# Window attention ahead of two gated MLPs: scores as four 64x64 tiles of TensorE's array, all eight heads of a token tile in one unit

## Chip, core and metric

One core of one Trainium2 chip. The metric is the device time of one execution in microseconds. The kernel before was run three times: 983.77, 983.69 and 981.26, median 983.69.

## What is computed

Attention over a sliding window of 64 tokens (4 batches, 8 heads, 576 tokens, head size 64), then two gated MLPs over the 2304 tokens (model size 512, hidden size 1536), all in float32. The reference, cut:

```python
def _attn_ref(q, k, v):
    scores = scale * np.matmul(q, k.transpose(0, 1, 3, 2))
    rel = pos[:, None] - pos[None, :]
    mask = (rel >= 0) & (rel < window)          # window = 64
    scores = np.where(mask, scores, -1000000000.0)
    ...                                         # softmax over the last axis
    return np.matmul(attn, v)

def _moe_ref(x, w_gate, w_val, w_out):
    gate = 1.0 / (1.0 + np.exp(-(x @ w_gate)))
    return gate * (x @ w_val) @ w_out

def _moe2_ref(x, w_a, w_b, w_out):
    return (x @ w_a) * (x @ w_b) @ w_out
```

## The kernel before

**Work.** The 2304 tokens are 18 token tiles of 128; two tiles make a block of 256 tokens (blocks 0 to 8). Blocks 0 to 4 (FRONT, in the groups 0, 1-2 and 3-4) go through the MLPs as plain products; blocks 5 to 8 (BACK) go through a scheme with seven products for eight in the second half of the program (`quad`, `bank_sum`), which the change does not touch. Each MLP weight is split into a high and a low part, and each product is three matmuls in fp32r. The weights arrive as 64-bit words that `decode` (L277) turns into the two parts: for each of the three pieces a, b, o of a chunk F it needs on ScalarE `low` (L285), `ex` (L288) and the high part (L303), on VectorE `wi`, `ex` and the low part, on GpSimd an addition (L296); the results are also stored to DRAM for the second half (`ka`, `kb`, `ko`, `kf`). There are 24 chunks.

**Attention before.** `attention(t, hq, dst, c0)` (L101) is one unit: token tile t, and half of the heads (hq 0 or 1, four heads), so 36 units. A query block of 64 tokens needs 128 keys: its own 64 and the 64 before, so a token tile of 128 queries has two halves s, and the key tile `kt` holds 64 + 128 columns. The steps of a unit, each ended by a `yield`:

1. load k, q, v of four heads (L110), four transposes on TensorE into one bank `kqps` (L119), which puts two heads on the 128 partitions (head parity e: partitions 0 to 63 and 64 to 127); evict `kt` (L121) and `qt` (L128). `qt` is zero padded: for each half s its 128 columns are 64 queries of the even head with zeros below, and 64 queries of the odd head with zeros above, so ScalarE writes it in two pieces of 64 partitions. Copies of v between partitions go by DMA to `vb` (L135, L139).
2. scores: four full matmuls into one bank, `sps[:, s, j, :] = qt[:, j, s]^T kt` (L146), 128 partitions (parity, query) by 128 keys.
3. and 4. for each s: mask and minimum on VectorE (L155), exp with the row sum on ScalarE (L160).
5. normalise on GpSimd (L169), four transposes `tps` (L172), evict `pt` (L174).
6. for the second half of the heads: attention times v, 16 matmuls of 128 rows by 64 columns with 64 moving columns into `xps` (L187), and the split of the result into `xh` and `xl` (L194, L195), or into `xq` (L198) for BACK blocks.

**Order.** `attention_stream` (L236) advances all live units in turn and starts a new one every `LAG` rounds. `attend(blk)` runs it until a block is done; in the middle of the program `attend(steps=...)` spreads the units of BACK evenly, by `STEPS`. `FIRST` (L442) says what has to be issued before the first products: attention of block 0, weights of chunks 0 and 1, attention of block 1, then products of block 0 with chunks 0 and 1, weights 2, attention 2, products of block 1, and so on. The framework then orders the instructions of each engine by its own timeline, so what is issued early in the program can stand later in an engine's queue. All DMAs are issued from SyncE's queue (SP).

**Memory.** PSUM has eight banks: two in `ps_acc` (tag acc), three in `ps_gv` (gv) and three in `ps_at` (at). `kqps`, `sps`, `tps` and `xps` come from `ps_at`, the first tiles' `kqps` from `ps_acc` and `sps` from `ps_gv`. The loaded words wait in three buffers of `stage`.

Of the kernel before, what the change touches and what calls it, by code (L numbers as in the profile page):

```python
# [9 lines left out]
F32 = mybir.dt.float32  # L10
# [10 lines left out]
def tile_window_attention_gated_mlps(ctx, tc, q, k, v, w1g, w1v, w1o, w2a, w2b, w2o, out):  # L21
# [14 lines left out]
    LAG = 1  # L36
# [18 lines left out]
    kts, vs, work, small = pool("kts", 5), pool("vs", 5), pool("work", 3), pool("small", 5)  # L55
# [10 lines left out]
    mask_0 = qp.tile([P, P], F32, name="mask_0")  # L66
# [12 lines left out]
    nc.vector.tensor_copy(mask_0, mask_n)  # L79
    nc.vector.memset(mask_0[:, 0:WIN], MASKED)  # L80


    lo, hi = slice(0, D), slice(D, P)
    before, own, last = slice(0, WIN), slice(WIN, KW), slice(P, KW)
    prev, held = {}, {}
# [15 lines left out]
    def attention(t, hq, dst, c0):  # L101
# [3 lines left out]
        heads = slice(4 * hq, 4 * hq + 4)  # L105
        raw = {}
        for nm, src in (("k", k), ("q", q), ("v", v)):
            r = (vs if nm == "v" else work).tile([P, 4, D], F32, tag=nm, name=f"{nm}{t}_{hq}")
            for off, n, b, s in runs(t * P, P):
                nc.sync.dma_start(out=r[off:off + n], in_=src[b, heads, s:s + n, :].rearrange("h s d -> s h d"))  # L110
            raw[nm] = r
# [3 lines left out]
        p_kq, p_s = (ps_acc, "acc") if t < 4 else (ps_at, "at"), (ps_gv, "gv") if t < 2 else (ps_at, "at")  # L115
# [4 lines left out]
        kt = kts.tile([P, 2, KW], F32, tag="kt", name=f"kt{t}_{hq}")  # L120
        nc.scalar.activation(out=kt[:, :, own], in_=kqps[:, 0], func=AF.Copy)  # L121
        if starts == [0]:
            nc.vector.memset(kt[:, :, before], 0.0)
        else:
            nc.gpsimd.tensor_copy(kt[:, :, before], prev["k", hq][:, :, last])
        qt = qts[(2 * t + hq) % len(qts)]
# [5 lines left out]
        prev["k", hq] = kt  # L132

        vb = work.tile([P, 4, D], F32, tag="vb", bufs=4, name=f"vb{t}_{hq}")
        nc.sync.dma_start(out=vb[hi], in_=raw["v"][lo])  # L135
        if starts == [0]:
            nc.gpsimd.memset(vb[lo], 0.0)
        else:
            nc.sync.dma_start(out=vb[lo], in_=prev["v", hq][hi])  # L139
        prev["v", hq] = raw["v"]  # L140
# [8 lines left out]
        yield  # L149
        ssum = small.tile([P, 2, 2], F32, tag="ssum", name=f"ssum{t}_{hq}")  # L150
        nmax = small.tile([P, 2, 2], F32, tag="nmax", name=f"nmax{t}_{hq}")
        pr = work.tile([P, 2, 2, P], F32, tag="pr", name=f"pr{t}_{hq}")
        for s in range(2):
            for j in range(2):
# [654 lines left out]
```

## Time and profile before

| | |
|---|---|
| median of 3 runs | 983.69 us (981.26 to 983.77) |
| profiled execution, its own time | 980.67 us |
| its span in the trace | 978.9 us |
| mean granted TensorE clock in the span | 0.997 of 2.4 GHz |

The profile is of a single execution. The span is the time from its first to its last instruction; the 1.8 us between span and time lie around the program. A matmul in float32 shows in the trace as two records on PE and two weight loads on PEld, one in fp32r as one. Starts of records are measured; the ends of matmuls are modelled, so the pace of TensorE is read from starts, or from the chain, in which each piece runs to the end of the last record in it.

### The profile page before, as it was taken

The numbers are of one execution on the slowest core, as the hardware profiler recorded it, in microseconds if no ns is written. First come the engines' busy times: TensorE is split into PE (matmuls) and PEld (weight loads), VectorE is DVE, ScalarE is ACT, GpSimd is POOL, SyncE is SP. The second block draws the span as 40 slices with busy tenths as digits, with TensorE's granted clock in tenths as the row PEclk, the third lists the DMA queues.
The fourth block names the chain that finished last, engine by engine and source line by source line (L and its number), as shares of the span: only waits on it lengthen the run. The fifth ranks groups of instructions, "written<-read, shape, count | busy, mean of one in ns | idle before, by whom it ended". The sixth has DMA issues, their size and how long they took to land.

```text
span 978.9 us, 15471 instructions
## 1 busy us (share of the span) xinstructions
PE 960.2 (98%) x5486; PEld 822.2 (84%) x5486; DVE 594.5 (61%) x1175; ACT 484.7 (50%) x1131; POOL 324.5 (33%) x351
## 2 busy tenths in 40 slices
PE   7799999999999999999999999999999999999998
PEld 6699998888888888888888888888888878888886
DVE  4788569776666794576575374445554674455645
ACT  7998666565454575654443233543332444322221
POOL 3543314332222221222121253543430485434300
PEclk9899999999999999999999999999999999999999
DMA  8999568675465573555462335544344564442312
GB/s 196 267 293 296 166 207 301 199 232 170 150 203 180 186 215 119 162 196 175 129 224 79 120 129 197 179 151 146 112 151 150 174 212 154 150 149 88 108 44 86
DMA packets 126524, 167.47 MB, mean 171 GB/s; under 512 B 63344, under 2 KB 92272, under 8 KB 126448
## 3 DMA queue, kind: packets, MB, share of 16 engines
q1 hardware_dynamic: 126448, 166.49, 53.1%
q8 instruction: 43, 0.70, 0.3%
q14 instruction: 33, 0.27, 0.1%
HBM read 106.95 MB, written 55.05 MB: 165 GB/s over the span
## 4 chain that ended last, share of the span: by engine, by line
PE 89%; ACT 4%; DVE 3%; DMA 1%; issue 1%; POOL 1%; SPq 0%; DVEq 0%; ACTq 0%; POOLq 0%
PE gps L320 16%; PE vps L320 16%; PE qa L609 13%; PE accq L669 13%; PE acc L363 8%; PE accm L408 7%; PE qb L609 6%; PE qc L609 3%; PE sps L146 2%; PE xps L187 2%; ACT pr L160 1%; PE tps L172 1%; PE kqps L119 1%; DMA kf<-ex 1%; ACT qt L128 1%
## 5 line engine op out<-in xcount | busy, mean ns | idle before, releaser
L296 POOL TENSOR_TENSOR wi<-wi,low 128x512 int32<-128x512 int32 x72 | 100.4, 1394 | 316.1 <-DVE wi L293 261.4
L320 PE MATMUL gps<-xh,wa 128*128 128x512 f32 (+1 forms) x624 | 175.6, 350 | 0.3 <-ACT xh L194 0.3
L320 PE MATMUL vps<-xh,wb 128*128 128x512 f32 (+1 forms) x624 | 169.4, 341 | 0.5 <-DVE wb L304 0.5
L594 POOL TENSOR_TENSOR wq<-s,wq 128x256 fp32r<-128x256 f32 x96 | 77.4, 810 | 147.1 <-ACT wq L593 147.0
L320 PEld LDWEIGHTS gps<-xh,wa 128*128 128x128 f32 x624 | 111.4, 191 | 13.9 <-ACT xh L194 0.5
L320 PEld LDWEIGHTS vps<-xh,wb 128*128 128x128 f32 x624 | 110.7, 189 | 14.3 <-DVE wb L304 0.7
L320 PE MATMUL gps<-xl,wa 128*128 128x512 f32 (+1 forms) x312 | 107.3, 344 | 1.1 <-DVE xl L195 1.1
L320 PE MATMUL vps<-xl,wb 128*128 128x512 f32 (+1 forms) x312 | 106.3, 341 | 0.0
L408 PE MATMUL accm<-hh,wo 128*128 128x256 f32 (+1 forms) x336 | 86.4, 332 | 0.0
L673 DVE TENSOR_TENSOR res<-accq,res 128x512 f32<-128x512 f32 x80 | 54.3, 687 | 49.0 <-PE accq L669 48.8
L627 ACT ACTIVATE r<-qa 128x512 f32<-128x512 f32 x72 | 42.6, 594 | 83.6 <-PE qa L609 80.3
L609 PE MATMUL qa<-op,wq 128*128 128x512 f32 x288 | 75.5, 390 | 0.7 <-POOL op L551 0.7
L363 PE MATMUL acc<-wo,hh 128*128 128x512 f32 x240 | 74.6, 392 | 1.4 <-DVE res L673 0.8
L609 PE MATMUL qb<-op,wq 128*128 128x512 f32 x288 | 73.4, 389 | 0.0
L330 DVE SCALAR_TENSOR_TENSOR hl<-hr,hh 128x512 fp32r<-128x512 f32 (+1 forms) x78 | 55.2, 708 | 24.2 <-ACT hh L329 23.9
L298 DVE SCALAR_TENSOR_TENSOR ex<-ex,wi 128x512 f32<-128x512 f32 x72 | 52.9, 735 | 24.6 <-ACT ex L288 13.1
L320 PEld LDWEIGHTS gps<-xl,wa 128*128 128x128 f32 x312 | 59.7, 191 | 7.4 <-DVE xl L195 1.3
L329 ACT ACTIVATE hh<-hr 128x512 fp32r<-128x512 f32 (+1 forms) x78 | 41.3, 529 | 48.8 <-DVE hr L347 30.9
L591 POOL TENSOR_TENSOR s<-wf 128x256 f32<-128x256 f32 x48 | 39.5, 822 | 76.7 <-DMA wf<-kf 75.0
L320 PEld LDWEIGHTS vps<-xl,wb 128*128 128x128 f32 x312 | 59.1, 189 | 6.9
L609 PEld LDWEIGHTS qa<-op,wq 128*128 128x128 f32 x288 | 53.9, 188 | 12.2 <-POOL op L551 1.1
L609 PEld LDWEIGHTS qb<-op,wq 128*128 128x128 f32 x288 | 54.1, 188 | 11.2
(125 smaller groups left out, 2031.8 us busy)
## 6 DMA issues: line engine op xcount, KB each, us to landing
wa<-ka SPq DMA_DIRECT2D x27, 512.0 KB, 3.2
wb<-kb SPq DMA_DIRECT2D x27, 512.0 KB, 3.8
wo<-ko SPq DMA_DIRECT2D x27, 512.0 KB, 4.4
st_o<-in_moe_w_out_dram SPq DMA_DIRECT2D x24, 512.0 KB, 4.2
kf<-ex SPq DMA_DIRECT2D x48, 256.0 KB, 4.0
ka<-wa SPq DMA_DIRECT2D x24, 512.0 KB, 3.0
kb<-wb SPq DMA_DIRECT2D x24, 512.0 KB, 3.5
ko<-wo SPq DMA_DIRECT2D x24, 512.0 KB, 3.2
```

The costliest lines, as they stand in the source:

```text
L296: nc.gpsimd.tensor_tensor(out=wi, in0=wi, in1=low, op=ALU.add)
L298: nc.vector.scalar_tensor_tensor(out=wf, in0=ex, scalar=SMALLEST, in1=wi.bitcast(F32), op0=ALU.is_ge, op1=ALU.mult)
L320: nc.tensor.matmul(ps, lhsT=a[:, c * P:(c + 1) * P], rhs=b[:, c, :], start=(n == 0), stop=(n == 3 * NP - 1))
L329: nc.scalar.activation(out=hh, in_=hr, func=AF.Copy, scale=factor)
L330: nc.vector.scalar_tensor_tensor(out=hl, in0=hr, scalar=factor, in1=hh.bitcast(F32), op0=ALU.mult, op1=ALU.subtract)
L363: nc.tensor.matmul(ps, lhsT=a[:, m * P:(m + 1) * P], rhs=b, start=begin and n == 0 and (phase == 1 or m % 2 == 0), stop=end and n == 2 and ...
L408: nc.tensor.matmul(ps[:, m], lhsT=a[:, sl], rhs=b, start=k == 0, stop=k == total - 1)
L594: nc.gpsimd.tensor_tensor(out=t[:, 1], in0=s, in1=t[:, 0].bitcast(F32), op=ALU.subtract)
L609: nc.tensor.matmul(ps, lhsT=a[:, c * P:(c + 1) * P], rhs=b[:, c, :], start=first and n == 0, stop=n == 5, skip_group_check=True,)
L627: nc.scalar.activation(out=r, in_=ps, func=AF.Copy)
L669: nc.tensor.matmul(ps, lhsT=a, rhs=b, start=n == 0, stop=n == len(pairs) - 1)
L673: nc.vector.tensor_tensor(out=dst, in0=ps, in1=dst, op=ALU.add)
```

## The change

The unit becomes a token tile with all eight heads (18 units, `LAG` 3, eleven steps). A load brings all eight heads (twice the bytes, half as many loads). The keys' transposes go to one bank, the queries' to another, and each is evicted in one ScalarE instruction of 128x512; the queries are no longer padded with zeros. The scores are 16 matmuls of 64 rows (one head's dimensions) by 64 columns (64 queries) with 128 moving columns (keys): the row half is the head's parity e, the column half is s, and the parities write to two banks, `sps[0]` and `sps[1]`. The partitions of the scores, the exps and `tps` are now (s, query) instead of (parity, query). The number and size of the instructions for mask, exp, normalising, transposes, `pt` and `xps` stay; the `xps` matmuls alternate between the two column halves one by one, instead of two by two. The mask for the first tile of a batch is made when it is needed (4 times), not once. Pools get new buffer counts. `STEPS` follows the new number of steps.

```diff
-    LAG = 1
+    LAG = 3
...
-    kts, vs, work, small = pool("kts", 5), pool("vs", 5), pool("work", 3), pool("small", 5)
+    kts, vs, work, small = pool("kts", 2), pool("vs", 3), pool("work", 2), pool("small", 2)
...
-    qts = [qp.tile([P, 2, 2, 2, WIN], F32, name=f"qt{i}") for i in range(2)]
-    for qt in qts:
-        nc.vector.memset(qt[hi, :, :, 0], 0.0)
-        nc.vector.memset(qt[lo, :, :, 1], 0.0)
+    def load_tile(nm, src, t, pool_of, tag, bufs):
+        r = pool_of.tile([P, H, D], F32, tag=tag, bufs=bufs, name=f"{nm}{t}")
+        for off, n, b, s in runs(t * P, P):
+            nc.sync.dma_start(out=r[off:off + n], in_=src[b, :, s:s + n, :].rearrange("h s d -> s h d"))
+        return r
...
-    def attention(t, hq, dst, c0):
+    def attention(t, dst, c0):
+        raw = [load_tile(nm, src, t, work, "kq", 3) for nm, src in (("k", k), ("q", q))]
+        v_own = load_tile("v", v, t, vs, "v", 3)
+        yield
-        kqps = p_kq[0].tile([P, 2, 2, P], F32, tag=p_kq[1], name=f"kqps{t}_{hq}")
-        for i, nm in enumerate("kq"):
-            for j in range(2):
-                nc.tensor.transpose(kqps[:, i, j, :], raw[nm][:, 2 * j:2 * j + 2, :], ident)
+        kqps = [kp.tile([P, NP, P], F32, tag=kq_tag, name=f"{nm}ps{t}") for nm in "kq"]
+        for ps, r in zip(kqps, raw):
+            for j in range(NP):
+                nc.tensor.transpose(ps[:, j, :], r[:, 2 * j:2 * j + 2, :], ident)
...
-        for e, rows in enumerate((lo, hi)):
-            nc.scalar.activation(
-                out=qt[rows, :, :, e], in_=kqps[rows, 1].rearrange("p j (s t) -> p j s t", s=2),
-                func=AF.Copy, scale=QSCALE,
-            )
+        qt = qp.tile([P, NP, P], F32, tag="qt", bufs=2, name=f"qt{t}")
+        nc.scalar.activation(out=kt[:, :, own], in_=kqps[0], func=AF.Copy)
+        nc.scalar.activation(out=qt, in_=kqps[1], func=AF.Copy, scale=QSCALE)
...
-        sps = p_s[0].tile([P, 2, 2, P], F32, tag=p_s[1], name=f"sps{t}_{hq}")
-        for s in range(2):
-            for j in range(2):
-                nc.tensor.matmul(
-                    sps[:, s, j, :], lhsT=qt[:, j, s], rhs=kt[:, j, s * WIN:s * WIN + P], start=True, stop=True
-                )
+        sps = [sp.tile([P, NP, P], F32, tag=s_tag, name=f"sps{t}_{e}") for e in range(2)]
+        for j in range(NP):
+            for turn in range(2):
+                for e, dims in enumerate((lo, hi)):
+                    s = (e + turn) % 2
+                    rows = slice(s * WIN, (s + 1) * WIN)
+                    nc.tensor.matmul(
+                        sps[e][rows, j, :], lhsT=qt[dims, j, rows], rhs=kt[dims, j, s * WIN:s * WIN + P],
+                        start=True, stop=True,
+                    )
...
-    STEPS = 4 * TB * 2 * 7 + 8
+    STEPS = len(BACK) * TB * 11 + 8
```

How the engines' queues change is shown at three places. In the names, `kt_0` and `qt_140` carry buffer numbers; `xN` is a run of equal instructions, and a matmul shown here is one instruction of the program (two records in the trace for float32).

TensorE, a unit's scores and the attention times v behind it, before: four full matmuls, two key and two query transposes, then `xps`.

```order
L146 MATMUL sps_0_1088<-kt_0_945,qt_140 128x128 x4
L119 MATMUL kqps_1_1099<-ident,k_1_1093 128x128 x2
L119 MATMUL kqps_1_1099<-ident,q_1_1095 128x128 x2
L187 MATMUL xps_1112<-pt_0_916,vb_0_623 64x64
L187 MATMUL xps_1112<-pt_0_916,v_0_610 64x64
```

The same place now, the last six of the 16 matmuls of a tile's scores:

```order
L138 MATMUL sps_0_814<-kt_795,qt_797 64x128
L138 MATMUL sps_1_815<-kt_795,qt_797 64x128
L138 MATMUL sps_0_814<-kt_795,qt_797 64x128
L138 MATMUL sps_1_815<-kt_795,qt_797 64x128
L138 MATMUL sps_0_814<-kt_795,qt_797 64x128
L138 MATMUL sps_1_815<-kt_795,qt_797 64x128
L186 MATMUL xps_834<-pt_0_809,vb_806 64x64
L186 MATMUL xps_834<-pt_1_810,vb_806 64x64
```

Two units of four matmuls have become 16 of a quarter of the array, and `xps` stands right behind them (so at 15 of the 18 tiles). Visits of TensorE to `xps`, between other work, fall from 24 to 20; visits to the tiled `sps` are 20.

SyncE's queue at the start of the program, before: the first weight load is the 28th DMA (digits behind k, q, v, vb are the token tile and the half of the heads).

```order
L110 DMA k3_0_493<-in_k_dram 128x4x64
L110 DMA q3_0_495<-in_q_dram 128x4x64
L110 DMA k3_1_539<-in_k_dram 128x4x64
L110 DMA q3_1_541<-in_q_dram 128x4x64
L271 DMA st_a_626<-in_moe_w_gate_dram 128x4x256
```

Now it is the seventh, and all three pieces of chunk 0 stand ahead of the queries of tile 1:

```order
L100 DMA k1_288<-in_k_dram 128x8x64
L100 DMA v1_292<-in_v_dram 128x8x64
L100 DMA v2_363<-in_v_dram 128x8x64
L268 DMA st_a_571<-in_moe_w_gate_dram 128x4x256
L268 DMA st_b_573<-in_moe_w_val_dram 128x4x256
L266 DMA st_o_575<-in_moe_w_out_dram 128x1024
L100 DMA q1_290<-in_q_dram 128x8x64
```

The decoding of weights has moved ahead of attention in the queue of loads.

ScalarE up to `xh` of token tile 3 (the input that block 1's first product waits for), before:

```order
L285 ACTIVATE low<-st_o 128x512
L160 ACTIVATE pr_0_924,ssum_0_922<-pr_0_924,nmax_0_923 128x128
L121 ACTIVATE kt_1_878<-kqps_1_873 128x2x128
L128 ACTIVATE qt_141<-kqps_1_873 64x4x64 x2
L160 ACTIVATE pr_0_924,ssum_0_922<-pr_0_924,nmax_0_923 128x128 x2
L303 ACTIVATE wb<-ex 128x512
L343 ACTIVATE hr<-gps 128x256
L160 ACTIVATE pr_0_924,ssum_0_922<-pr_0_924,nmax_0_923 128x128
L194 ACTIVATE xh_1_353<-xps_888 128x4x128
```

And now:

```order
L282 ACTIVATE low<-st_a 128x512
L300 ACTIVATE wo<-ex 128x512
L383 ACTIVATE gacc_1219<-accm 128x512 x2
L285 ACTIVATE ex<-st_a 128x512
L282 ACTIVATE low<-st_b 128x512
L285 ACTIVATE ex<-st_b 128x512
L300 ACTIVATE wa<-ex 128x512
L153 ACTIVATE pr_0_857,stat_856<-pr_0_857,stat_856 128x128 x4
L153 ACTIVATE pr_1_858,stat_856<-pr_1_858,stat_856 128x128
L192 ACTIVATE xh_1_343<-xps_834 128x4x128
```

The first of these rows reads the first piece of chunk 3 (the fourth `st_a`). Up to `xh` of tile 3 the queue held 6 `low`, 5 `ex`, 5 high parts, 12 `kt`, 24 `qt` and 44 exps; it now holds 11 `low`, 11 `ex`, 10 high parts, 6 `kt`, 6 `qt`, 45 exps and 2 `gacc`.

## Rows read from the trace of the kernel before

**Rows 1.** The page's first part: busy time of TensorE and ScalarE.

```profile
PE 960.2 (98%) x5486; PEld 822.2 (84%) x5486; DVE 594.5 (61%) x1175; ACT 484.7 (50%) x1131; POOL 324.5 (33%) x351
```

**Rows 2.** Windows: stretch, length, each engine's busy time (records), clock, DMA share, GB/s.

```profile
0.00:25.00 25.00, 19.59 (x146) 16.24 (x147) 10.64 (x70) 19.32 (x68) 9.67 (x25) 1.00 0.81 196
25.00:55.00 30.00, 23.21 (x225) 21.24 (x224) 23.68 (x81) 28.73 (x91) 16.53 (x15) 0.89 0.94 272
55.00:100.00 45.00, 45.00 (x444) 43.89 (x443) 37.69 (x117) 41.23 (x127) 20.00 (x20) 1.00 0.98 297
100.00:150.00 50.00, 50.00 (x461) 48.08 (x460) 29.99 (x67) 30.74 (x74) 12.27 (x13) 1.00 0.64 191
150.00:500.00 350.00, 349.44 (x2070) 301.37 (x2069) 236.82 (x505) 196.40 (x456) 92.09 (x79) 1.00 0.59 187
```

**Rows 3.** Waits of ScalarE, first 55 us: waited for, us in total, times, longest.

```profile
ACT kt L121 <- PE kqps L119: 3.7, 1, 3.7
ACT ex L288 <- DMA kf<-ex: 1.0, 1, 1.0
ACT pr L160 <- DVE nmax L155: 0.8, 1, 0.8
```

**Rows 4.** Chain that ended last, 96 to 104 us: start, us, what, records.

```profile
100.12 0.72 PE accm L408 x6
100.84 0.89 PE sps L146 x8
101.74 0.44 PE kqps L119 x4
102.17 1.13 PE xps L187 x32
```

**Rows 5.** The same chain, 60 to 66 us.

```profile
62.52 0.66 PE xps L187 x16
```

**Rows 6.** Timeline of TensorE, 100.8 to 103.3 us: start, us, line, operands, records merged.

```profile
101.79 0.38 PE L119 MATMUL kqps<-ident,q 128*128 128x128 f32 x2
102.11 0.34 PE L187 MATMUL xps<-pt,vb 128*64 128x64 f32 x4
102.97 0.33 PE L187 MATMUL xps<-pt,v 128*64 128x64 f32 x4
103.23 0.38 PE L408 MATMUL accm<-hh,wo 128*128 128x256 f32 x1
```

**Rows 7.** Chain, 15 and 24 us: ScalarE's steps back to back.

```profile
15.64 0.76 ACT pr L160 x4
16.40 0.27 ACT kt L121
16.67 0.27 ACT qt L128
...
16.96 0.38 ACT qt L128
...
17.36 0.40 ACT pr L160
...
23.93 0.49 ACT pt L174
24.42 0.56 ACT low L285
24.98 0.56 ACT ex L288
```

**Rows 8.** Timeline of ScalarE, 51 to 60 us, around `xh` of tile 3.

```profile
53.60 0.59 ACT L194 ACTIVATE xh<-xps 128x512 fp32r<-128x512 f32 x1
...
57.22 0.41 ACT L329 ACTIVATE hh<-hr 128x256 fp32r<-128x256 f32 x1
57.53 0.38 ACT L121 ACTIVATE kt<-kqps 128x256 f32<-128x256 f32 x1
...
59.07 0.62 ACT L303 ACTIVATE wo<-ex 128x512 fp32r<-128x512 f32 x1
59.59 0.38 ACT L343 ACTIVATE hr<-gps 128x256 f32<-128x256 f32 x1
```

**Rows 9.** Timeline of TensorE, 53 to 56 us: last wait of the start, block 1's first product.

```profile
54.54 0.51 PE L320 MATMUL vps<-xh,wb 128*128 128x256 f32 x2 [0.49 <-DVE wb L304]
55.84 0.28 PE L320 MATMUL gps<-xh,wa 128*128 128x256 f32 x1
55.96 0.28 PE L320 MATMUL vps<-xh,wb 128*128 128x256 f32 x1
```

**Rows 10.** Timeline of SyncE, 14.5 to 20 us: issues of loads.

```profile
15.75 0.46 SPq L110 DMA_DIRECT2D q<-in_q_dram  x1
16.26 0.50 SPq L271 DMA_DIRECT2D st_a<-in_moe_w_gate_dram  x1
```

**Rows 11.** Waits of TensorE, 100 to 560 us.

```profile
PE acc L363 <- DVE gacc L388: 0.6, 1, 0.6
```

More of the change, by code (lines that the diff above doesn't have):

```diff
@@ L65, in tile_window_attention_gated_mlps @@
     mask_n = qp.tile([P, P], F32, name="mask_n")
-    mask_0 = qp.tile([P, P], F32, name="mask_0")
     nc.gpsimd.memset(mask_n, 0.0)
@@ L149, in attention @@
[L149 to L154, printed above, removed]
-                nc.vector.tensor_tensor_reduce(
-                    out=pr[:, s, j, :], in0=sps[:, s, j, :], in1=mask_0 if s in starts else mask_n,
-                    scale=1.0, scalar=LARGEST, op0=ALU.add, op1=ALU.min, accum_out=nmax[:, s, j:j + 1],
-                )
-            for j in range(2):
+            nc.gpsimd.tensor_copy(kt[:, :, before], prev["k"][:, :, last])
@@ new lines, in attention @@
+        yield
+        stat = small.tile([P, 3, 2, NP], F32, tag="stat", name=f"stat{t}")
+        ssum, nmax, den = (stat[:, i] for i in range(3))
+        pr = [work.tile([P, NP, P], F32, tag="pr", bufs=4, name=f"pr{t}_{e}") for e in range(2)]
+        for e in range(2):
+            for j in range(NP):
+                nc.vector.tensor_tensor_reduce(
+                    out=pr[e][:, j, :], in0=sps[e][:, j, :], in1=mask,
+                    scale=1.0, scalar=LARGEST, op0=ALU.add, op1=ALU.min, accum_out=nmax[:, e, j:j + 1],
+                )
+            for j in range(NP):
@@ L167, in attention @@
-        nc.vector.reciprocal(out=den, in_=den)
-        tps = ps_at.tile([P, 2, 2, P], F32, tag="at", name=f"tps{t}_{hq}")
-        nc.gpsimd.tensor_tensor(out=pr, in0=pr, in1=den.unsqueeze(3).to_broadcast([P, 2, 2, P]), op=ALU.mult)
-        for s in range(2):
-            for j in range(2):
-                nc.tensor.transpose(tps[:, s, j, :], pr[:, s, j, :], ident)
-        pt = work.tile([P, 2, 4, WIN], F32, tag="pt", bufs=2, name=f"pt{t}_{hq}")
-        nc.scalar.activation(
-            out=pt.rearrange("p s i t -> p (s i t)"), in_=tps.rearrange("p s j t -> p (s j t)"), func=AF.Copy
-        )
@@ L177, in attention @@
-        yield
-        both = held.setdefault(t, [])
-        both.append((vb, raw["v"], pt))
-        if hq == 0:
-            return
+        v_before = work.tile([P, H, D], F32, tag="vb", name=f"vb{t}")
+        nc.sync.dma_start(out=v_before[hi], in_=v_own[lo])
+        if starts == [0]:
+            nc.gpsimd.memset(v_before[lo], 0.0)
+        else:
+            nc.sync.dma_start(out=v_before[lo], in_=prev["v"][hi])
+        prev["v"] = v_own
+        pt = [work.tile([P, NP, P], F32, tag="pt", bufs=2, name=f"pt{t}_{e}") for e in range(2)]
@@ new lines, in attention @@
+        for e in range(2):
+            nc.vector.tensor_scalar(out=den[:, e], in0=ssum[:, e], scalar1=1.0e-9, scalar2=None, op0=ALU.add)
+            nc.vector.reciprocal(out=den[:, e], in_=den[:, e])
+            nc.gpsimd.tensor_tensor(
+                out=pr[e], in0=pr[e], in1=den[:, e].unsqueeze(2).to_broadcast([P, NP, P]), op=ALU.mult
+            )
+            yield
+        for e in range(2):
+            tps = ps_at.tile([P, NP, P], F32, tag="at", name=f"tps{t}_{e}")
+            for j in range(NP):
+                nc.tensor.transpose(tps[:, j, :], pr[e][:, j, :], ident)
+            nc.scalar.activation(out=pt[e], in_=tps, func=AF.Copy)
+            yield
```

64 lines of the change are left out of this document (24 added, 40 removed).

## Prediction

> **What bounds the kernel now.** The page's first part and the windows come first. TensorE is busy 960.2 of 978.9 us [rows 1], and the windows say where the rest is [rows 2]: from 55 to 150 us it never pauses, from 150 to 500 us it is busy 349.44 of 350. In the first 55 us it is busy 19.59 and 23.21 us, so 12.2 us of idleness lie there, before the stream of products is full. There ScalarE sets the pace: it is busy 28.73 of the 30 us from 25 to 55, and its waits in the whole start are three, 5.5 us together, the largest the wait for the first transposes [rows 3]. The DMA engines come right behind, with shares of 0.81, 0.94 and 0.98. So a microsecond saved on TensorE is a microsecond of the end where its stream is full, and nothing before; and what happens in the start counts by one moment: when block 1's first product can begin, 55.84 us [rows 9], since TensorE has not waited after 54.54. It needs `xh` of token tile 3, which starts on ScalarE at 53.60 and takes 0.49 until the next step can start (so 54.1) [rows 7, 8]. The sum is therefore made in two terms: the shift of that moment, and the change of TensorE's work behind it.
>
> **Scores on TensorE.** A unit's four matmuls are 8 records in 0.89 us [rows 4], so a token tile costs 1.78 and a record 0.111. Now it is 16 matmuls, 32 records with the same 128 moving columns. Alone, 32 records would take 3.55; if all four quarters of the array work side by side, 0.89. The nearest row is `xps`: its records use two column halves. 16 records more cost 1.13 - 0.66 = 0.47 us [rows 4, 5], 0.029 each, while a record with half of the moving columns would take 0.055 alone. So two column halves do run side by side, at nearly twice the pace. Row halves side by side are in no row. I take 32 x 0.029 = 0.94 for the records, since weight loads have been seen to follow each other that fast.
>
> Entering and leaving the tiled array costs something. The last transpose before `xps` starts at about 101.90 (the second of two from 101.79, 0.11 apart) and `accm` at 103.23 [rows 6]; less the transpose's own 0.11 this visit took 1.22 us, less 32 x 0.029 it is 0.28. The last record is longer now (128 moving columns, not 64), so I add 0.08: 0.94 + 0.28 + 0.08 = **1.30 us** a tile, 0.48 saved. Bounds: 1.17 (0.89 and the visit) and, if only pairs run side by side, 16 x 0.111 + 0.28 = 2.06. No overlap at all would be 3.83.
>
> The Trainium skill (TensorEngine Tiling (Array Packing), "Key Properties") has the rule that changing the tiling mode drains TensorE, which speaks against this change. The visit's 0.28 us agrees with it; the page gives no price.
>
> Behind block 1's first product there stood 25 units of scores (22.25 us); now 12 tiles (15.6): -6.65. `accm` records ahead of it are 24, not 6, at 0.72/6 = 0.12 [rows 4]: -2.2 behind it. Four more transposes at 0.11 stand ahead: -0.4. Of the places where `xps` follows the scores directly, 11 lie behind it; if going from one tiling to the other costs one change instead of two, that is 11 x 0.14 = -1.5 (bounds 0 and -3.1); two `xps` visits fewer and two split score visits cancel. **TensorE's work behind the moment: -10.7 us.**
>
> **ScalarE up to the moment.** `kt` and `qt` of a unit cost 0.96 us (16.40 to 17.36); an eviction of 128x512 costs 0.49 (`pt`) [rows 7]. Twelve units were 11.5 us, six tiles are 12 x 0.49 = 5.9: -5.6. But the new order puts more of the weights' decoding ahead: 5 `low` and 6 `ex` at 0.56 [rows 7], 5 high parts at 0.52 (59.07 to 59.59) [rows 8], 2 `gacc` at 0.49, an exp at 0.38 [rows 7], an `hh` at 0.31 (57.22 to 57.53) [rows 8]: +10.4. Net +4.8: by ScalarE's own work the moment moves from 54.1 to 58.9.
>
> **DMA up to the moment.** Before, the first weight load was issued at 16.26 us [rows 10]; now it is seventh in SyncE's queue. Up to the fourth `st_a`, which ScalarE reads 6.7 us of work before the end of `xh` of tile 3 (`low`, `wo`, 2 `gacc`, `ex`, `low`, `ex`, `wa`, 5 exps, `xh`), the queue holds 18 tile loads of 0.262 MB, 10 weight loads and 6 stores of 0.524, 5 stores of 0.262 and 7 copies of 0.131: 15.3 MB. At full share the DMA engines moved 196/0.81 = 242, then 272/0.94 = 289 and 303 GB/s [rows 2]: 6.05 MB by 25 us, 14.7 by 55, so 15.3 MB by 57.0. At the rates as they were, 4.9 MB by 25 and 13.1 by 55, it is 62.5. ScalarE would come to that `low` at 52.2 and wait. I take 57.0, as issues are fewer and larger and SyncE no longer needs a slot of half a microsecond [rows 10] for every 128 KB. Then `xh` ends at 63.7, and block 1's first product starts 7.9 us later than before. The half-empty TensorE costs nothing there.
>
> **The rest.** Mask, exp, normalising, `pt` and `xps` keep number and size. Four mask copies and fewer `kt` copies lie under ScalarE's work (VectorE is busy 37.69 and GpSimd 20.00 of 45 us [rows 2]); without that cover they would cost below 2 us together. In BACK TensorE has waited 0.6 us in all from 100 to 560 us [rows 11]; scores now need two banks at once out of three, and I leave this at 0, up to +2. Less work on ScalarE after 60 us is worth nothing, as TensorE is full.
>
> **Sum.** +7.9 - 10.7 = -2.8 us. The profiled execution's own time was 980.67, 3.0 under the median of the runs; the same difference against the median, 983.69, gives **980.9 us**. About 0.3% (3 us) is what a measurement of this kernel can tell from no change, so this stands just at that limit.
>
> **Rivals.**
>
> *Weights in time.* The DMAs keep up with ScalarE (for it: loads start in the first 5 us instead of at 16; against it: shares of 0.94 and more already). The moment is 58.9, +3.1, and the sum -7.6: 976.1. With the scores at 1.17 it reaches -9 and below.
>
> *Loads take back the gain.* SyncE's queue is first in, first out for weights and token tiles: queries of tile 1 now wait behind all of chunk 0. If the DMA engines do no better than their measured rates, the fourth `st_a` lands at 62.5, the product starts at 69.2, +13.4, and the sum is +2.7: 986.4, slower. It decides from a landing at about 59.8 us on, where the product would start 10.7 us late.
>
> *Quarters only in pairs.* If the row halves take turns, a tile's scores cost 2.06; behind the moment that is 12 x 2.06 - 22.25 = +2.5 instead of -6.65, and the sum 7.9 + 2.5 - 4.1 = +6.3: 990.0. For it: no row shows row halves together. Against it: `xps` runs at nearly the full pace of its two halves, and the two parities write to different banks.
> The Trainium skill (TensorE: Matmul & The Clock Gate, "The mechanism") says that a weight load overlaps running matmuls only if its row group differs, which would keep the two column halves of a parity apart and also leave pairs. The trace disagrees for `xps`, whose tiles share all rows and still go at 0.029 us a record. By the speedup that the same page gives ("Measured speedup vs the span model") for four row tiles of another shape, 3.07 times, an estimate for the records is 3.55/3.07 = 1.16 us instead of 0.94, or 12 x 0.22 = 2.6 us more in the sum.
>
> **Chances.** The forecast 0.45 (its own range 977 to 985; 0.22 faster, 0.21 same, 0.02 slower), weights in time 0.22 (0.21 faster, 0.01 same), loads take back the gain 0.20 (0.05 same, 0.15 slower), pairs 0.13 (0.01 same, 0.12 slower). Together: faster 0.43, same 0.28, slower 0.29. The range reaches from the better half of the second case to the third and the middle of the fourth: 971 to 991.
>
> **What would show it.** In the new trace: a tile's 32 score records in about 1.0 us from first to last start (1.8 would be pairs); ScalarE waiting for `st_a` of chunk 3 at 53 to 57 us; block 1's first `gps` near 64 us, and no TensorE wait of note after it; more than 12 us of TensorE idleness in the first 65 us. It is wrong if the product starts before 59 us or after 67, if the scores cost over 1.5 us a tile, or if TensorE waits for score inputs in the BACK part.

## The result and the profile after

The changed kernel takes **987.36 us** (median of 6 runs, 986.24 to 989.69) where the kernel before, in the same comparison, takes 982.92 (980.37 to 984.08): a ratio of 1.0053, 95% interval 1.0034 to 1.0073. It is slower by half a per cent, where 980.9 us and a slight gain were forecast. The time lies within the forecast's range of 971 to 991, but on the other side of no change. The profiled execution took 987.0 us, with a span of 984.9, against 980.67 and 978.9; the two profiled executions lie 6.3 us apart and the medians 4.4, so what is added up from the two traces comes out some 2 us larger than the change of the medians.

The page's first part, which answers to [rows 1]:

```profile
PE 954.0 (97%) x5774; PEld 809.1 (82%) x5774; DVE 591.0 (60%) x1175; ACT 465.3 (47%) x1059; POOL 321.0 (33%) x333
```

Every engine has less to do, and the kernel is slower; so the time is lost in waits. The windows, for the stretches and columns of [rows 2]:

```profile
0.00:25.00 25.00, 14.67 (x113) 12.18 (x114) 12.54 (x45) 13.63 (x35) 10.56 (x20) 0.85 1.09 259
25.00:55.00 30.00, 21.59 (x269) 18.49 (x267) 26.03 (x83) 24.61 (x77) 16.46 (x14) 0.73 1.04 312
55.00:100.00 45.00, 40.20 (x449) 37.16 (x448) 32.17 (x118) 37.71 (x117) 19.59 (x18) 0.96 0.92 267
100.00:150.00 50.00, 50.00 (x548) 48.45 (x548) 25.71 (x80) 27.28 (x77) 9.50 (x9) 1.00 0.47 136
150.00:500.00 350.00, 348.59 (x2186) 295.93 (x2185) 232.72 (x504) 190.57 (x430) 89.05 (x71) 1.00 0.60 187
```

From 100 us on nothing of size has changed. The loss is in the first three stretches. TensorE is busy less (and at a lower granted clock, 0.85 and 0.73 in the first two, so it also works more slowly), while ScalarE fell from 19.32 and 28.73 us to 13.63 and 24.61: the engine that set the pace before is no longer full. In the chain of waits up to block 1's first product it held 34.5 us before and holds 7.5 now. The end of the start, in the timeline of TensorE (answers to [rows 9]; in brackets the wait ahead and what ended it):

```profile
68.91 0.58 PE L317 MATMUL gps<-xh,wa 128*128 128x256 f32 x1 [1.11 <-ACT xh L192]
69.29 0.42 PE L317 MATMUL vps<-xh,wb 128*128 128x256 f32 x1
```

Block 1's first product starts at 68.91 us instead of 55.84, **13.1 us later** (7.9 were forecast). From there to the end of the span it is 916.0 us instead of 923.0, **7.0 us less** (10.7 were forecast). The difference of the spans is the sum, +6.0. The waits of ScalarE in the first 69 us, against [rows 3]:

```profile
ACT pr L153 <- DVE stat L148: 6.1, 4, 2.4
ACT kt L125 <- PE kps L118: 3.7, 1, 3.7
ACT low L282 <- POOL wi L293: 3.7, 5, 2.3
...
ACT low L282 <- DMA st_a<-in_moe_w_gate_dram: 0.8, 1, 0.8
```

ScalarE waits for VectorE and GpSimd, and hardly for the weights' loads. In the chain of waits VectorE holds 14.2 of the 28 us from 41 to 69; it does the masks of the scores (`pr`) and the decoding (`wi`, `ex`, `wa`, `wb`, `wo`) in one queue, with GpSimd's `wi` in between (3.0 us). Another 7.2 us are two transfers, the store of a decoded piece (`kf<-ex`) and a load of queries. Pieces of it:

```profile
44.10 0.59 DVE wo L301
44.70 0.60 DVE wi L290
...
45.48 1.26 POOL wi L293
46.76 1.52 DVE ex L295
48.30 0.63 DVE wi L287
48.93 3.73 DMA kf<-ex
...
58.17 3.46 DMA q<-in_q_dram
...
66.86 0.20 DVE pr L148
67.07 0.34 DVE wi L287
67.41 0.60 DVE wa L301
68.01 0.60 DVE wi L290
```

Ahead of 41 us the chain is another: 16.9 us of it are transfers, the first weights (5.4) and two loads of keys:

```profile
17.98 6.32 DMA k<-in_k_dram
...
25.78 5.17 DMA k<-in_k_dram
```

That is why loads had to be tested as a cause besides the decoding.

Which decoding stands ahead of which operand is seen in ScalarE's timeline, where each of the weights' pieces begins with one `low` and each token tile ends with one `xh`:

```profile
30.07 0.66 ACT L282 ACTIVATE low<-st_b 128x512 int32<-128x512 uint32 x1
34.63 0.65 ACT L282 ACTIVATE low<-st_o 128x512 int32<-128x512 uint32 x1
36.73 0.57 ACT L192 ACTIVATE xh<-xps 128x512 fp32r<-128x512 f32 x1
...
61.58 0.70 ACT L282 ACTIVATE low<-st_a 128x512 int32<-128x512 uint32 x1
64.69 0.68 ACT L282 ACTIVATE low<-st_b 128x512 int32<-128x512 uint32 x1 [0.35 <-POOL wi L293]
68.28 0.57 ACT L192 ACTIVATE xh<-xps 128x512 fp32r<-128x512 f32 x1
```

Six of the `low` stand ahead of the first operand and eleven ahead of the fourth. In the kernel before it was none and six: its first `low` starts at 24.3 us, behind its first `xh`, here in its chain of waits:

```profile
23.34 0.60 ACT xh L194
```

The scores themselves, in the timeline of TensorE (answers to [rows 6]):

```profile
100.67 0.40 PE L317 MATMUL gps<-xh,wa 128*128 128x256 f32 x2
101.00 1.10 PE L138 MATMUL sps<-kt,qt 64*64 64x128 f32 x32
102.03 0.34 PE L186 MATMUL xps<-pt,vb 128*64 128x64 f32 x4
```

A tile's 32 records take 1.03 us up to the next piece. Record by record, four of them start within 20 ns (101.000, 101.006, 101.013 and 101.020), the next four 160 ns after these, and from then on such rounds of four follow each other every 109 ns. A record doesn't say on which quarter it runs; but one at a time the 32 would have taken 3.55 us, so more than three must have run at once, and that takes all four quarters.

### The profile page after: what moved, and what is told of

Its sections match the earlier page's. It is cut to its first block, busy times and chain, and to the rows that moved or that the text cites. A ratio compares the mean times of both kernels' runs of the same rounds, so it can differ in the third digit from the quotient of the medians.

```text
span 984.9 us, 15767 instructions
## 1 busy us (share of the span) xinstructions
PE 954.0 (97%) x5774; PEld 809.1 (82%) x5774; DVE 591.0 (60%) x1175; ACT 465.3 (47%) x1059; POOL 321.0 (33%) x333
## 4 chain that ended last, share of the span: by engine, by line
PE 80%; DVE 7%; DMA 6%; ACT 2%; issue 2%; POOL 2%; SPq 1%; DVEq 0%; POOLq 0%; ACTq 0%
PE gps L317 14%; PE vps L317 13%; PE qa L606 13%; PE accq L666 13%; PE acc L360 8%; PE qb L606 6%; PE accm L405 5%; PE qc L606 3%; DMA kf<-ex 3%; PE xps L186 1%; PE sps L138 1%; DMA k<-in_k_dram 1%; DVE ex L295 1%; PE tps L178 1%; POOL wi L293 1%
## 5 line engine op out<-in xcount | busy, mean ns | idle before, releaser
L293 POOL TENSOR_TENSOR wi<-wi,low 128x512 int32<-128x512 int32 x72 | 102.8, 1428 | 306.8 <-DVE wi L290 251.3
L317 PE MATMUL vps<-xh,wb 128*128 128x512 f32 (+1 forms) x624 | 171.4, 342 | 0.0
L317 PEld LDWEIGHTS vps<-xh,wb 128*128 128x128 f32 x624 | 111.2, 190 | 13.8
L295 DVE SCALAR_TENSOR_TENSOR ex<-ex,wi 128x512 f32<-128x512 f32 x72 | 53.0, 735 | 46.0 <-ACT ex L285 20.7
L327 DVE SCALAR_TENSOR_TENSOR hl<-hr,hh 128x512 fp32r<-128x512 f32 (+1 forms) x78 | 53.3, 684 | 22.7 <-ACT hh L326 22.5
L405 PEld LDWEIGHTS accm<-hh,wo 128*128 128x128 f32 x336 | 57.8, 190 | 8.0 <-DVE gacc L385 2.1
L606 PEld LDWEIGHTS qa<-op,wq 128*128 128x128 f32 x288 | 53.9, 188 | 12.2 <-POOL op L548 1.1
```

The source lines that it names most:

```text
L293: nc.gpsimd.tensor_tensor(out=wi, in0=wi, in1=low, op=ALU.add)
L295: nc.vector.scalar_tensor_tensor(out=wf, in0=ex, scalar=SMALLEST, in1=wi.bitcast(F32), op0=ALU.is_ge, op1=ALU.mult)
L317: nc.tensor.matmul(ps, lhsT=a[:, c * P:(c + 1) * P], rhs=b[:, c, :], start=(n == 0), stop=(n == 3 * NP - 1))
L327: nc.vector.scalar_tensor_tensor(out=hl, in0=hr, scalar=factor, in1=hh.bitcast(F32), op0=ALU.mult, op1=ALU.subtract)
L405: nc.tensor.matmul(ps[:, m], lhsT=a[:, sl], rhs=b, start=k == 0, stop=k == total - 1)
L606: nc.tensor.matmul(ps, lhsT=a[:, c * P:(c + 1) * P], rhs=b[:, c, :], start=first and n == 0, stop=n == 5, skip_group_check=True,)
```

## The experiments

T is the start of block 1's first product. Theory **L**: the loads make it late, since weights stand ahead of token tiles in a full DMA queue. **B**: the loads of k and q do, which rotate through three buffers. **U**: the whole-tile unit does, being long itself. **D**: the decoding does, which the new order puts ahead of the attention. **C**: TensorE's half clock in the sparse start does. The first four runs weigh L against U; the other theories came up after them.

The medians and ratios come from the runs, each kernel against runs of the kernel before on the same chip (medians 982.0 to 982.9); the rest of the table is worked out from the traces. "Steps" are the decoding steps (`low`) that started on ScalarE ahead of tile 3's `xh`; "half" is the time before T in which the granted clock stood at its lower level (1.2 GHz). TensorE's idleness is counted up to its last matmul, and a wait that ends at T is counted before T. Each trace is of one execution, and the executions of one kernel differ by 1 to 6 us, so a difference of a microsecond or two in T between two rows is not shown to be the edit's.

| kernel | median, us | ratio to before, 95% interval | first `xh` ends | steps | T | T to end of span | TensorE idle before / behind T | half |
|---|---|---|---|---|---|---|---|---|
| before | 982.92 | | 23.9 | 6 | 55.8 | 923.0 | 12.2 / 2.8 | 6.8 |
| after | 987.36 | 1.0053 (1.0034 to 1.0073) | 37.3 | 11 | 68.9 | 916.0 | 23.2 / 4.1 | 24.0 |
| hold_q1 | 990.25 | 1.0081 (1.0068 to 1.0094) | 34.0 | 11 | 74.0 | 912.5 | 25.5 / 2.7 | 41.0 |
| hold_q2q3 | 986.95 | 1.0045 (1.0033 to 1.0057) | 36.3 | 10 | 70.6 | 915.2 | 23.1 / 4.0 | 34.1 |
| before_tiled | 987.86 | 1.0051 (1.0037 to 1.0064) | 21.9 | 7 | 55.4 | 927.9 | 12.3 / 4.3 | 10.2 |
| lag2 | 1007.19 | 1.0252 (1.0238 to 1.0265) | 42.9 | 14 | 81.9 | 922.7 | 30.5 / 7.4 | 41.5 |
| early_kq | 987.26 | 1.0050 (1.0035 to 1.0065) | 30.3 | 9 | 67.2 | 916.7 | 20.3 / 6.6 | 30.7 |
| hybrid | **978.54** | **0.9964 (0.9950 to 0.9978)** | 20.8 | 5 | 49.9 | 925.3 | 9.7 / 9.0 | 6.8 |
| hold_x3 | 987.63 | 1.0048 (1.0030 to 1.0066) | 37.6 | 6 | 64.7 | 922.5 | 20.7 / 9.0 | 27.3 |
| hybrid6 | 982.23 | 1.0000 (0.9987 to 1.0013) | 21.4 | 7 | 57.4 | 926.2 | 12.5 / 7.4 | 17.1 |
| behind | 982.78 | 1.0007 (0.9997 to 1.0017) | 30.7 | 6 | 62.7 | 918.3 | 18.2 / 5.1 | 27.3 |
| behind_kq | 988.17 | 1.0066 (1.0048 to 1.0083) | 30.5 | 6 | 63.9 | 922.3 | 22.7 / 7.5 | 20.5 |
| behind_fill | 995.03 | 1.0127 (1.0105 to 1.0148) | 33.9 | 6 | 71.7 | 921.3 | 5.5 / 5.5 | 0 |
| behind_fill2 | 987.75 | 1.0051 (1.0036 to 1.0067) | 31.7 | 6 | 65.1 | 922.7 | 13.8 / 8.3 | 13.7 |

### Loads of the weights held back (hold_q1, hold_q2q3)

A weight buffer's first touch is a one-element copy on GpSimd that needs the queries of a later tile, so the load cannot be issued ahead of them.

```diff
+    HOLD = {0: 1}            # hold_q2q3: {0: 2, 1: 3}
...
+            if F in HOLD:
+                nc.gpsimd.tensor_copy(r[0:1, 0:1, 0], queries[HOLD[F]][0:1, 0, 0:1].bitcast(I32))
```

> Each weight buffer of chunk 0 is first touched by a one-element copy from the queries of token tile 1, so that chunk 0's weight loads are issued after those queries have landed; nothing else differs from the changed kernel. Theory L (the late start comes from the loads: weights stand ahead of the token tiles in a DMA queue that is full): block 1's first product starts at 62 to 65 us instead of 68.9, the time falls to 981 to 984. Theory U (it comes from the unit of a whole tile: long steps, few in flight): no change, 986 to 989.

> As hold_q1, but chunk 0 waits for the queries of tile 2 and chunk 1 for those of tile 3. Theory L: block 1's first product at 56 to 61 us, 975 to 980. Theory U: 986 or more, since the decoding comes later and the units are as long as before.

Neither gained what L asks for: T came 5.1 and 1.7 us later still, and hold_q1 is slower than U had it too. With the token tiles' loads ahead of the weights' the first operand was earlier by 3.3 and 1.0 us and the fourth was not. The holding copy itself makes GpSimd wait for the queries (5.0 us in hold_q1, 2.0 in hold_q2q3), which may have cost part of a gain; but in the changed kernel ScalarE waits for weights 0.8 us in all. **L falls as the main cause.**

### The kernel before with quarters, and the changed one with LAG 2

before_tiled keeps the units of four heads and changes only the queries (not padded) and the scores (16 matmuls of 64 by 64, a bank per parity).

```diff
-                nc.tensor.matmul(
-                    sps[:, s, j, :], lhsT=qt[:, j, s], rhs=kt[:, j, s * WIN:s * WIN + P], start=True, stop=True
-                )
+            for turn in range(2):
+                for e, dims in enumerate((lo, hi)):
+                    s = (e + turn) % 2
+                    rows = slice(s * WIN, (s + 1) * WIN)
+                    nc.tensor.matmul(
+                        sps[e][rows, j, :], lhsT=qt[dims, j, rows], rhs=kt[dims, j, s * WIN:s * WIN + P],
+                        start=True, stop=True,
+                    )
```

> The kernel before, units of four heads, LAG 1, its buffers and loads, with one part of the change alone: queries without padding (one eviction a unit), scores as four 64x64 tiles, a bank per parity. A unit has 16 records, so by 0.029 a record and 0.28 to 0.36 a visit it costs 0.75 to 0.83 us instead of 0.89: 36 x 0.06 to 0.14 is 2 to 5 us less TensorE work. ScalarE saves one step of 0.39 a unit, some 12 units up to block 1's first product: the start up to 4 us earlier. Theories L and U both: 975 to 981. If tiled scores themselves cost (drains, banks), 984 or more.

T stayed, so neither the quarters nor the plain queries delay the start; but the stretch behind it became 4.9 us longer, the expectation's last case. Timeline of TensorE in this kernel, one visit to the scores:

```profile
103.45 0.28 PE L406 MATMUL accm<-hh,wo 128*128 128x256 f32 x1
103.66 0.67 PE L143 MATMUL sps<-kt,qt 64*64 64x128 f32 x16
104.25 0.39 PE L406 MATMUL accm<-hh,wo 128*128 128x256 f32 x1
```

Sixteen records take 0.59 us where eight padded ones took 0.89 [rows 4], but the step into them takes 0.21. Over all visits behind T the last record ahead of the scores is charged 0.278 us instead of 0.192 (27 visits in both kernels), and a score record followed by a product 0.199 instead of 0.030 (17 in both), so a visit costs about 0.26 us more than a padded one. That eats the records' own gain (attention and the steps into it are 1.5 us longer behind T, not shorter); 1.5 us of waits and some 2 us that I could not assign make up the rest of the 4.9. In the changed kernel there are 14 visits behind T, eleven of them of 32 records, and it is the longer visit that pays.

lag2 is the changed kernel with `LAG = 2`, so that more units are under way at once.

> The changed kernel with LAG 2, so that attention units start closer together; the first 18 issues of SyncE stand in the same order, weights of chunk 0 ahead of the queries of tile 1. Theory L: no change to speak of, 985 to 989. Theory U: block 1's first product at 62 to 65 us, 980 to 983.

T moved the other way, by 13 us, and with it the time. More units in flight do not help; three more steps of decoding stand ahead of tile 3. This row started theory D. It does not price it: at what behind shows below (6.2 us for five steps) three steps would be some 4 us, and the other 9 are not explained.

### Early loads of k and q; small units at the start

early_kq loads keys and queries of the first four tiles into four buffers of `accp` that are idle until the first results. hybrid uses units of four heads, one step apart, for tiles 0 to 3, with the changed kernel's buffers and quarters, and whole tiles from tile 4 on.

```diff
+        if t < EARLY:            # 4
+            raw = accp.tile([P, 2, 2, N], F32, tag="xacc", name=f"kq{t}").rearrange(
+                "p i j (h d) -> p i (j h) d", d=D)
```

```diff
+                if t < HALVES:   # 4 in hybrid, 6 in hybrid6
+                    for hq in range(2):
+                        yield 1, blk, half_heads(t, hq, x[0, (blk,)], i * P)
+                else:
+                    yield LAG, blk, attention(t, x[0, (blk,)], i * P)
```

> The changed kernel, but keys and queries of the first four token tiles are loaded into four buffers that lie idle until the first results (those of gacc), so their loads wait for no transposes; nothing else moves. Theory B (the start is late because k and q rotate through three buffers: each load waits for a transpose and then needs 5 to 6 us to land, as the chain shows from 6 to 31 us): block 1's first product at 58 to 63 instead of 68.9 us, 978 to 982 us. Theory D (the start is late because VectorE's queue, with the decoding of the weights in it, is the chain from 41 us on): the product stays at 66 to 70, 985 to 989 us.

> Units of four heads, one step apart, for the first four token tiles (with the unpadded queries and the four quarters), whole tiles from the fifth on, in the changed kernel's buffers. Theory U (the late start comes of the long steps of whole tiles at the start alone): block 1's first product at 55 to 58 as before, and behind it 915 to 918 us as in the changed kernel, so 972 to 977 us, below both kernels. Theory B (three k and q buffers and the loads' latency): the same buffers hold the same bytes, the product comes at 62 or later, 980 us or more.

early_kq: the first operand came 7.0 us earlier, T 1.7, and the time did not move. The early loads also changed the order (the first weight load is issued at 17.0 us instead of 6.2, and two steps of decoding instead of six stand ahead of the first operand), so the 7.0 us are not of the loads alone. **B falls** as the cause of the late T: with the loads out of the way the chain of waits goes through the decoding, as here at 46 to 50 us:

```profile
46.94 0.44 DVE wi L294
47.40 0.70 DVE wi L297
...
48.24 1.60 POOL wi L300
49.86 0.69 DVE ex L302
50.55 0.20 DVE pr L155
```

hybrid beats both kernels: 0.9964 (0.9950 to 0.9978) of the time before. T is 19.0 us ahead of the changed kernel's, with the same buffers and bytes, and earlier than the 55 to 58 that U asked for:

```profile
49.90 0.36 PE L420 MATMUL gps<-xh,wa 128*128 128x256 f32 x1
```

ScalarE's timeline shows the order back at what it was before, the first operand ahead of all decoding:

```profile
20.22 0.59 ACT L291 ACTIVATE xh<-xps 128x512 fp32r<-128x512 f32 x1
20.72 0.69 ACT L385 ACTIVATE low<-st_a 128x512 int32<-128x512 uint32 x1
25.98 0.71 ACT L385 ACTIVATE low<-st_b 128x512 int32<-128x512 uint32 x1
29.10 0.61 ACT L291 ACTIVATE xh<-xps 128x512 fp32r<-128x512 f32 x1
```

It missed its 972 to 977 since the stretch behind T is 925.3 us, not 916. TensorE waits 4.9 us more there, and work that the changed kernel did during its longer start now lies behind T (18 records of `accm`, 10 of `vps`, transposes).

> Units of four heads for the first six token tiles instead of four, whole tiles from the seventh on. Theory D: tile 3 has the same five to seven decoding steps ahead of it, block 1's first product within 3 us of the 49.9 of the kernel with four such tiles; TensorE's waits for tiles 4 and 5 between 50 and 105 us (some 5 us) become shorter, but their scores are read in two more visits each: 976 to 980 us. Theory U: the waits from 50 to 105 us go, 973 to 976 us.

With two more tiles in small units T went back to 57.4, for seven steps of decoding ahead of it and more of tiles 4 and 5 in between. Neither column of the expectation held: T was not within 3 us, and the time was above both. (The trace is of an execution of 985.4 us, 3.2 above the median of this kernel's runs, so T may be earlier in others.) Where the units change size is itself a setting of the order.

### The decoding held back (hold_x3, behind, behind_kq)

hold_x3 lets nothing of chunk 2 be loaded before tile 3's operand is done. behind ties four decoding steps to the operands, by a one-element copy on ScalarE, which does both anyway, so it waits for no other engine. It holds back no load by itself, but a weight's buffer comes free only when its step is done: the fourth weight load is issued at 32.3 us instead of 15.6. In both, chunk 1's decoding or all weights stand behind block 1's attention in the program.

```diff
+            if F == 2:                                      # hold_x3, in load_weights
+                nc.gpsimd.tensor_copy(r[0:1, 0:1, 0], x[0, (1,)][0][0:1, 0, P:P + 1].bitcast(I32))
```

```diff
+    BEHIND = {(0, 0): 0, (0, 2): 1, (1, 1): 2, (2, 0): 3}   # behind, in decode: step -> token tile
...
+            if (F, i) in BEHIND:
+                blk, half = divmod(BEHIND[F, i], TB)
+                nc.scalar.activation(
+                    out=low[0:1, 0:1], in_=x[0, (blk,)][0][0:1, 0, half * P:half * P + 1].bitcast(F32), func=AF.Copy
+                )
```

> The changed kernel, but the buffers of chunk 2's weights are first touched by a one-element GpSimd copy of the operand of token tile 3, so that nothing of chunk 2 is loaded or decoded before block 1's operands are done; chunk 1 stands behind block 1's attention in the program. On ScalarE six decoding steps instead of ten then stand ahead of tile 3's operand. Theory D (the late start is the decoding of later chunks, which the order puts ahead of the attention on VectorE, GpSimd and ScalarE; the traces show 6, 7, 11 and 14 decoding steps before block 1's first product where it starts at 49.9, 55.8, 68.9 and 81.9 us, some 4 us a step): the product starts at 52 to 60, and the kernel takes 976 to 984 us, with TensorE waiting later for chunk 2. Theory U (the whole-tile units are themselves too slow at the start, and the decoding only fills their waits): the product stays at 65 or later, 986 us or more.

> The changed kernel's whole-tile units and loads, but four decoding steps are set behind the operands of token tiles 0 to 3 on ScalarE (one element of the operand is first copied into the step's buffer), and both blocks' attention stands ahead of the weights in the program. Ahead of the four operands 0, 2, 4 and 6 decoding steps then stand on ScalarE, as in the kernel before, instead of 6, 7, 9 and 11. Theory D (the start is late because the order puts the decoding ahead of the attention): operands done near 24, 33, 44 and 54 us as before, block 1's first product at 52 to 59, 972 to 979 us. Theory U (a unit of a whole tile takes longer from load to operand, whatever stands beside it): the first operand at 28 or later and the product at 62 or later, 981 us or more.

> As the kernel with the decoding set behind the operands, and the keys and queries of the first four tiles loaded into four idle buffers besides, so that no load waits for a transpose. Theory D alone: the same as without the buffers, within 2 us. Theory B with it (once the decoding is out of the way, the loads are what is late next): block 1's first product 3 us or more earlier than without the buffers, 2 us or more off the time. Theory U: the product at 60 or later here too.

hold_x3: T came 4.3 us earlier with 6 steps instead of 11, all of it behind 46 us, since the first six steps still stand ahead of tile 0. T, 64.7, is far from D's 52 to 60 and just under U's 65, and the time did not follow. Chunk 2 was issued late, and TensorE was idle for 9.0 us behind T, not 4.1; 1.4 of them are a wait for a decoded weight (`wa`), most of the others fall on the attention and on `accm`:

```profile
65.47 0.37 SPq L270 DMA_DIRECT2D st_a<-in_moe_w_gate_dram  x1
```

behind has the order of before, 0, 2, 4 and 6 steps ahead of the four operands. ScalarE and TensorE:

```profile
30.10 0.58 ACT L193 ACTIVATE xh<-xps 128x512 fp32r<-128x512 f32 x1
31.05 0.18 ACT L285 ACTIVATE low<-xh 1x1 int32<-1x1 f32 x1
31.62 0.67 ACT L288 ACTIVATE low<-st_a 128x512 int32<-128x512 uint32 x1
```

```profile
62.67 0.28 PE L323 MATMUL gps<-xh,wa 128*128 128x256 f32 x1
```

T is 6.2 us earlier than in the changed kernel, and the time is back at that of the kernel before (1.0007, 0.9997 to 1.0017). So **D is shown for 6.2 of the 13.1 us.** The weights' loads came later with the order; but in hold_q2q3, where they were held back and ten steps stayed ahead of tile 3, T did not gain. By its own bounds the expectation came out in U's column (first operand after 28, T after 62, over 981 us), since the other 6.8 us (62.7 against 55.8) remain with the same order: the first operand of a whole tile is done at 30.7 us with no decoding ahead of it, where two small units did it by 23.9. That is U's part. hybrid supports it: with the same buffers and quarters, small units and 0, 2, 4 and 5 steps ahead of the operands, T is 12.8 us earlier than here. The two shares are rough: counted at the end of the fourth `xh` (54.2, 68.9 and 61.8 us in before, after and behind) they are 7.0 and 7.7.

behind_kq adds the early loads and gains nothing on T (63.9), and its time is 5 us longer, with the weights' first load issued at 18.1 us behind sixteen other loads and two copies: B does not explain the rest.

### TensorE's clock (behind_fill, behind_fill2)

In the start of behind TensorE is at its lower level for 27.3 us, and its chain of waits up to T runs through TensorE for 26.6 us, 17.1 of them at that level (in the kernel before 7.0 and none). Two pieces of it, at the lower level, where 32 such records take 1.03 us at the upper one:

```profile
18.02 1.99 PE sps L139 x32
...
24.52 2.05 PE sps L139 x32
```

Products of the identity matrix, written into banks that are overwritten anyway, fill its waits.

```diff
+    def fill(t, ps):
+        for _ in range(FILL if t < 4 else 0):               # 6, and 2 in behind_fill2
+            nc.tensor.matmul(ps, lhsT=ident, rhs=ident, start=True, stop=True)
...
+        fill(t, sps[0][:, 0, :])                            # and ahead of kps, qps, tps and xps
```

> The kernel with the decoding set behind the operands, and six products of the identity matrix (some 1.3 us at full clock) ahead of each group of transposes, scores and products with v of the first four tiles, written into the bank that the group then overwrites, so that TensorE works through its waits. Theory C (what is left of the late start is TensorE at half clock: ten steps of TensorE on the chain of the first 60 us take twice as long, 4 to 5 us in all): no or hardly any half clock before the product, the product 3 us or more ahead of the 62.7 us without the filling, below 60, and 978 to 981 us. Theory U (the length of a whole-tile unit on VectorE, ScalarE, GpSimd and the loads): the clock rises, but the product stays at 62 or later, the filling itself being in the way, and the time at 982 us or more.

> As the kernel with the filling, with two products of the identity ahead of each group instead of six: some 13 us of TensorE in the first 60 us instead of 38, against 18 us in which it stood idle without any. Theory C (TensorE at half clock is what is left of the late start): the clock full for most of the start and the product at 60 or earlier, 981 us or less. Theory U (the length of a whole-tile unit): with the clock full and the filling small enough for the waits, the product still at 62 to 66, 982 to 986 us.

Windows of behind and then of behind_fill, 0 to 55 us (columns as above):

```profile
0.00:25.00 25.00, 14.06 (x122) 11.62 (x126) 6.94 (x48) 13.80 (x44) 7.12 (x19) 0.84 0.95 205
25.00:55.00 30.00, 22.70 (x263) 19.80 (x258) 22.43 (x83) 22.95 (x77) 14.69 (x14) 0.73 0.81 229
```

```profile
0.00:25.00 25.00, 23.53 (x227) 22.90 (x228) 6.40 (x44) 10.89 (x34) 5.74 (x17) 1.00 0.93 195
25.00:55.00 30.00, 27.48 (x348) 25.58 (x347) 15.78 (x73) 21.56 (x70) 12.66 (x12) 1.00 0.70 189
```

Six products keep the clock full (1.00) up to T and are themselves in the way: T is 9.0 us later. Two halve the time at the lower level (13.7 us) and T is 2.4 us later, not earlier; its time, 987.75, is longer than U had it too. C did not show itself, but it is not refuted: the filling has its own cost, which no run separates. At the upper level the 17.1 us would take half, so the clock could account for up to 8.5 us (an estimate from these two numbers), more than the 6.8 that remain.

## Why the prediction was wrong

**The moment.** It was the right quantity to watch: the whole result is +13.1 at T and -7.0 behind it. The forecast's +7.9 came from two steps, and both fail.

*ScalarE up to the moment.* The prediction saw that the new order puts more decoding ahead, and priced it on ScalarE alone: +10.4 for it, -5.6 for the evictions, +4.8 net, which was 3.1 at T. That carries over from the kernel before that ScalarE is full [rows 2]. ScalarE's work up to T did grow, by 2.9 us (48.9 to 51.8); but its waits grew from 6.2 (the 5.5 of the prediction and one of 0.7 at the very start) to 17.1, and a step of decoding costs what it costs in the queues of VectorE (two `wi`, an `ex`, a low part) and GpSimd (one `wi` of some 1.4 us), in which the masks and the normalising stand too. Up to T the decoding grew from 15.7 to 30.7 us on VectorE and from 8.3 to 14.6 on GpSimd. This is the failed step, the decoding priced on ScalarE alone, and behind prices it: 6.2 us. "Four mask copies and fewer `kt` copies lie under ScalarE's work" is the same misreading: the cover was taken for granted on the engine that had stopped setting the pace.

*DMA up to the moment.* The bytes were right: 259 and 312 GB/s in the first two windows make 15.8 MB by 55 us, against the 15.3 by 57.0 of the forecast. But ScalarE's waits for `st_a` are 0.8 us in all, at the first chunk, and the fourth `st_a`, issued at 49.9 us and landed at 54.9, ahead of the forecast's 57.0, was read at 61.6 without a wait. So the 4.8 us that the prediction added for the loads were not lost there. They were lost, with 2 more, in a cause that the prediction had no term for: the 6.8 us that units of all eight heads take longer to the moment when the order is that of before, TensorE's lower clock included.

**TensorE behind the moment.** Right in its parts, short in the sum. Charging each record the time to the next start, waits over 0.15 us taken out, the attention fell by 8.4 us (56.4 to 48.0): scores -7.0 with the last score record's way out (forecast -6.65), `xps` -1.0 (-1.5), transposes -0.4 (-0.4); `accm` ahead of T -2.5 (-2.2). A tile's scores at 1.08, and 0.15 more on the way in, agree with the forecast of 1.30; the scores of 24 units stood behind the moment before, not 25, so the same prices would have given -5.8. Together -10.9 against -10.7. Given back: 2.7 us in `gps` and `vps`, of which 3.4 us at half clock from 68.8 us on cost about 1.7, and 1.1 us more waits, where the prediction had none. That leaves -7.1, where -7.0 were measured.

**The rivals.** *Loads take back the gain* came within 1 us of the result, 986.4 with the product at 69.2, and its mechanism did not occur: it had the fourth `st_a` land at 62.5, and it landed at 54.9; its number was right by chance. *Weights in time* was half true: the weights were there when they were read, and it did not help. *Quarters only in pairs* is refuted by the rounds of four records 6 to 7 ns apart. The Trainium skill (TensorE: Matmul & The Clock Gate, "The mechanism") says that a weight load overlaps running matmuls only where its row group differs. The trace disagrees: the four records of a round, which by their pace need all four quarters and so include column halves that share their rows, started within 20 ns, and the weight loads of the next round started 53 to 73 ns after the first record of a round that lasted 160.

**The signs that were named.** Of the four, the scores at about 1.0 us and the idleness of over 12 us (20.7 in the first 65) came. The wait for chunk 3's `st_a` did not, and the product started after 67, which the prediction had named as what would make it wrong. TensorE's waits in BACK stayed small (1.2 us at `accm`).

**Still open.** Which step of the whole-tile unit makes up the 6.8 us was not separated. Early loads of k and q did not recover it; how much of it is TensorE's lower clock (27.3 us in behind), no run shows.

## What to carry to other kernels

When a change alters the order that a scheduler makes, count the work that it puts ahead of the critical operand on every engine of the chain, not only on the one that was full before: an engine that loses load also loses its power to hide the others. Units that save visits in a full stream can be too long for a start that lives by interleaving; here small units for the first four tiles and large ones behind them beat both kernels. A cheaper tiled matmul pays by the visit: at 0.26 us more to get in and out than a plain one, 16 short records did not gain and 32 did.

## What was not expected of the hardware

- With matmuls on the four 64x64 quarters, alternating in rows and columns, records started in rounds of four, 6 to 7 ns apart, and the next round 109 ns after (160 after the first): 32 records in 1.03 us with the way out, where one at a time at 0.111 they would have taken 3.55.
- A sparse TensorE falls to its lower level (1.2 GHz) often: 24.0 us of the first 69 in the changed kernel, against 6.8 of the first 56. The same 32 score records took 1.92 us there up to the next piece (39.28 to 41.20). What this costs depends on the chain: in the changed kernel only 5.1 us of the chain up to T are TensorE at the lower level, in behind 17.1.
